# A gated linear-attention kernel: most of the first x rows transposed by the DMA engines instead of TensorE

## Chip, cores and metric

The kernel runs on one core of a Trainium2 chip. The metric is the device time of one execution in microseconds (us). Three runs of the kernel before gave a median of 188.91 us (188.75 to 189.58).

## The reference

Two linear-attention blocks A and B read the same input x (2048 rows, 640 columns, bf16) with their own weights, and a gate computed from x mixes their outputs. Cut to what matters:

```python
def block(x, wqkv, wo):                       # 32 heads of 20
    q, k, v = heads(x @ wqkv)
    phi = lambda t: where(t > 0, t + 1, exp(t)) + 1e-6
    pq, pk = phi(q), phi(k)
    kv = einsum("bhsd,bhse->bhde", pk, v)
    z  = einsum("bhsd->bhd", pk)
    num = einsum("bhqd,bhde->bhqe", pq, kv)
    den = einsum("bhqd,bhd->bhq", pq, z) + 1e-6
    return merge(num / den) @ wo

g = sigmoid((A_x * gate_w).sum(-1))
out = g * block(A_x, A_wqkv, A_wo) + (1 - g) * block(A_x, B_wqkv, B_wo)
```

## The kernel before

The 2048 rows of x are held twice in SBUF. `xn` has them as 16 chunks of 128 rows, rows on partitions. `xT` is x transposed, five slices of 128 columns by 2048 rows, columns on partitions. Products that sum over the 640 columns (k and q) read `xT`; products that sum over the rows (x transposed by phi(k), called g in the tile names) read `xn`.

The order of the work, for block A first and then for B, is: k for every chunk (`kA`: ten matmuls, two halves of 320 columns by five slices), phi on ScalarE and VectorE, q by weight slices (`qA`), the g products with Strassen-like sums, the normaliser, and then small weight products. At the end, pairs of row chunks make the output. Most of it lies in blocks under `tc.manual_schedule()`, where each engine's instructions stand in the order in which they are written.

The front of the kernel is where the change lies.

- **Loads (lines 113 to 141).** The first 512 rows of x are loaded by `load_x` as four chunks, `xn[:, 0]` to `xn[:, 3]`, in turn on SP's and ScalarE's queue. Chunk q holds the rows 4p + q (the view `xb0`), so these four chunks are interleaved. The k weights of A (`wkA`, five slices) come by `load_wk`, three transfers on SP and one on ScalarE. The q weights (`wqA`, lines 134 to 136) come in two transfers on SP. Behind all of these, SP issues 15 transposing transfers (line 139): for each of the row groups 512 to 1023, 1024 to 1535 and 1536 to 2047, five slices of 512 rows by 128 columns go straight into `xT`.
- **Warm-up and the gate weights (lines 168 to 178).** Seven matmuls on constants come first on TensorE. Then the gate weight row, five rows of 128, is transposed (`gcol`, line 174), copied by VectorE (`gsb`, line 176), and put by GpSimd (POOL) as a column 640 into each slice of `wkA` (line 178). The second half of each k product of A is therefore 321 columns wide, and its last column is the gate logit.
- **First k chunks (`k_first`, line 252).** For chunks 0 to 3, `x_transpose` (line 213) makes five TensorE transposes into PSUM and two VectorE copies into `xT`. All 20 transposes stand ahead of the 40 matmuls (`k_mm`, line 234), which go slice by slice: slice 0 for the four chunks, slice 1 for the four, and then slices 2 to 4 chunk by chunk, each followed by `k_done` (phi and the logit).
- **What follows (line 729).** q of rows 0 to 511 (`q_block` twice, `q_single`), k of chunks 4 to 7, q of rows 512 to 1023, k of chunks 8 to 15, and the remaining q. Chunks 4 to 7 read the first five of the 15 transposes. After these, SP loads `xn` for the chunks 4 to 15 (line 737), then `wv`, `wo` and B's k weights.
- **PSUM.** `ps_raw` hands out four slots of two banks each. A tile that takes a slot over waits for the readers of the tile before it. Before the change, the warm-up and the gate column are in slot 3, the transposes in slots 0 and 1, and the k products of chunks 0 to 3 in slots 2, 3, 0 and 1.
- **Output rows.** `rows_of` (line 598) sends chunks 0 to 3 to the interleaved rows and the others to plain ones.

Of the kernel before, what the change touches and what calls it, by code (L numbers as in the profile page):

```python
# [8 lines left out]
P = 128  # L9
FP32 = mybir.dt.float32  # L10
BF16 = mybir.dt.bfloat16
# [3 lines left out]
S, D, H = 2048, 640, 32  # L15
Dh = D // H
DT = D // P
ST = S // P
NB = 4
CB = 4  # L20
HB = 512
# [12 lines left out]
def kernel(  # L34
# [11 lines left out]
    nc = tc.nc  # L46
    x2 = A_x.flatten_outer_dims()
    out2 = out.flatten_outer_dims()
# [3 lines left out]
    wpool = ctx.enter_context(tc.tile_pool(name="wpool", bufs=1))  # L52
    work = ctx.enter_context(tc.tile_pool(name="work", bufs=2))
# [6 lines left out]
    def ps_raw(name, slot=None):  # L60

        if slot is None:
            slot = turn[0]
            turn[0] = (slot + 1) % 4
        return psum.tile([P, 4 * HB], BF16, tag=f"ps{slot}", name=name)

    def ps(name, slot=None):

        return ps_raw(name, slot).bitcast(FP32).rearrange("p (b n) -> p b n", b=2)

    xT = persist.tile([P, DT, S], BF16, name="xT")
    xn = persist.tile([P, ST, D], BF16, name="xn")
# [6 lines left out]
    ident = persist.tile([P, P], BF16, name="ident")  # L79
# [26 lines left out]
    wq_dram = [A_wqkv.rearrange("(c p) f -> p c f", p=P), B_wqkv.rearrange("(c p) f -> p c f", p=P)]  # L106
# [3 lines left out]
    nc.vector.memset(ones[:], 1.0)  # L110
    nc.vector.memset(KVT[:], 0.0)
    nc.vector.memset(lift[:], 1.0 + EPS)
    xb0 = x2[0:CB * P, :].rearrange("(p q) d -> p q d", q=CB)
    wk = [None, None]
    wv = [None, None]
    wq = [None, None]
    wk[0] = wpool.tile([P, DT, D + 16], BF16, tag="wk", name="wkA")
    def load_x(eng, lo, hi):
        eng.dma_start(out=xn[:, lo:hi, :], in_=xb0[:, lo:hi, :])

    def load_wk(eng, lo, hi):
        eng.dma_start(out=wk[0][:, lo:hi, 0:D], in_=wq_dram[0][:, lo:hi, D:2 * D])

    grow, logitT = R[0:DT, 0, 2, 0:P], R[:, 0, 1, 0:P]
    nc.scalar.dma_start(out=grow, in_=gate_w.rearrange("(c p) -> c p", p=P))
    load_x(nc.sync, 0, 1)
    load_x(nc.scalar, 1, 2)
    load_x(nc.sync, 2, 3)
    load_x(nc.scalar, 3, 4)
    load_wk(nc.sync, 0, 1)  # L130
    load_wk(nc.scalar, 1, 2)
    load_wk(nc.sync, 2, 3)
    load_wk(nc.sync, 3, DT)
    wq[0] = wpool.tile([P, DT, D], BF16, tag="wq", name="wqA")
    for lo, hi in ((0, 2), (2, DT)):
        nc.sync.dma_start(out=wq[0][:, lo:hi, :], in_=wq_dram[0][:, lo:hi, 0:D])
    for n in range(1, NB):
        for c in range(DT):
            nc.sync.dma_start_transpose(
                out=xT[:, c, n * HB:(n + 1) * HB], in_=x2[n * HB:(n + 1) * HB, c * P:(c + 1) * P]  # L140
            )


    make_identity(nc, ident[:])
    for r in range(4):
        rows = slice(32 * r, 32 * r + 32)
        nc.gpsimd.tensor_copy(out=I4[rows], in_=ident[rows, rows])
    nc.gpsimd.tensor_copy(
        out=spread[:].rearrange("p (h t) -> p h t", t=TW), in_=I4[:, :, None].to_broadcast([P, H, TW])
    )  # L150
    nc.gpsimd.tensor_tensor(
        out=I16[0:2 * ST], in0=ident[0:2 * ST, 0:ST], in1=ident[0:2 * ST, ST:2 * ST], op=ALU.add
    )
    nc.gpsimd.memset(maskE[:], 1.0)
    for sign, base in ((1, 0), (-1, Dh - 1)):
        nc.gpsimd.affine_select(
            out=maskE[:], in_=maskE[:], pattern=[[-sign * Dh, WB[0] // Dh], [0, Dh]],
# [3 lines left out]
    for sign, base in ((1, 0), (-1, TW - 1)):  # L161
        nc.gpsimd.affine_select(
            out=headE[:], in_=headE[:], pattern=[[-sign * TW, H]],
# [1 line left out]
        )  # L165


    raw = ps_raw("warm", 3)
    warm = raw.bitcast(FP32).rearrange("p (b n) -> p b n", b=2)
    one_l, one_r = [nc.const_aps.tensor(1.0, [P, n], BF16) for n in (P, HB)]  # L170
    for k in range(7):
        nc.tensor.matmul(warm[:, 0, :], lhsT=one_l, rhs=one_r, start=True, stop=True)  # L172
    gcol = raw[:, 2 * HB:2 * HB + DT]
    nc.tensor.transpose(out=gcol, in_=grow, identity=ident[0:DT, 0:DT])
    gsb = work.tile([P, DT], BF16, tag="rT", name="gsb")
    nc.vector.tensor_copy(out=gsb[:], in_=gcol)
    for c in (0, 1, 2, 4, 3):
        nc.gpsimd.tensor_copy(out=wk[0][:, c, D:D + 1], in_=gsb[:, c:c + 1])

    def by_group(dst, lhsT, src, h):  # L180

        for c in range(DT):
            for j in range(4):
                r0 = h * 2 * HB + j * RB
                nc.tensor.matmul(
                    dst[32 * j:32 * j + 32, :], lhsT=lhsT[:, c, :], rhs=src[:, c, r0:r0 + RB],
                    start=(c == 0), stop=(c == DT - 1), tile_position=(0, 32 * j),
                )
# [20 lines left out]

    def gate_done(b):  # L210
        nc.vector.tensor_scalar(ge[b][:], ge[b][:], 1.0, 1e30, op0=ALU.add, op1=ALU.min)

    def x_transpose(i, pt, cuts=(0, DT)):
        for c in range(DT):
            nc.tensor.transpose(out=pt[:, c * P:(c + 1) * P], in_=xn[:, i, c * P:(c + 1) * P], identity=ident[:])  # L215
        src = pt[:, 0:D].rearrange("p (c n) -> p c n", c=DT)
        for lo, hi in zip(cuts, cuts[1:]):
            nc.vector.tensor_copy(out=xT[:, lo:hi, i * P:(i + 1) * P], in_=src[:, lo:hi])  # L218

    def phi(dst, src, n, lifted=False, side=None):  # L220

        e = work.tile([P, src.shape[1], n], BF16, tag="e", name="e", bufs=3)
        nc.scalar.activation(out=e[:], in_=src, func=ACT.Exp)  # L223
        if side is not None:
            side()
        if lifted:
            nc.scalar.activation(out=dst, in_=src, func=ACT.Identity, bias=lift[:])
        nc.vector.tensor_scalar(e[:], e[:], 1.0, EPS, op0=ALU.min, op1=ALU.add)  # L228
        if lifted:
            nc.vector.tensor_tensor(out=dst, in0=dst, in1=e[:], op=ALU.max)  # L230
            return
        nc.vector.scalar_tensor_tensor(out=dst, in0=src, scalar=1.0 + EPS, in1=e[:], op0=ALU.add, op1=ALU.max)  # L232

    def k_mm(b, i, c, pt, hf):
        w = HF + (hf if b == 0 else 0)
        nc.tensor.matmul(  # L236
            pt[:, hf, 0:w], lhsT=xT[:, c, i * P:(i + 1) * P], rhs=wk[b][:, c, hf * HF:hf * HF + w],
            start=(c == 0), stop=(c == DT - 1),
        )

    def k_done(b, i, pt):
        side = (lambda: nc.scalar.copy(out=logit[:, i:i + 1], in_=pt[:, 1, HF:HF + 1])) if b == 0 else None
        phi(pk[:, i, :].rearrange("p (b n) -> p b n", b=2), pt[:, :, 0:HF], HF, side=side)

    def k_chunk(b, i, slot=None):
        pt = ps(f"k{'AB'[b]}", slot)
        for hf in range(2):
            for c in range(DT):
                k_mm(b, i, c, pt, hf)
        k_done(b, i, pt)  # L250

    def k_first():

        pts = [ps("kA", 2 + i) for i in range(2)]
        raw = [ps_raw("xt", i) for i in range(2)]

        def part(i, cs):
            for c in cs:
                for hf in range(2):
                    k_mm(0, i, c, pts[i], hf)  # L260

        for i in range(4):
            x_transpose(i, raw[i % 2][:, i // 2 * 2 * HB:], (0, 2, DT))
        for i in range(2):
            part(i, (0,))
        pts += [ps("kA", i) for i in range(2)]
        for i in range(2, 4):
            part(i, (0,))
        for i in range(4):
            part(i, (1,))  # L270
        for i in range(4):
            part(i, (2, 3, 4))
            k_done(0, i, pts[i])

    def mixed(t, m):
# [320 lines left out]
        nc.vector.tensor_tensor(out=pqT[b][:, m, :], in0=pqT[b][:, m, :], in1=rec, op=ALU.mult)  # L596

    def rows_of(i):
        n, q = divmod(i, CB)
        rows = out2[n * HB:(n + 1) * HB, :]  # L600
        return rows.rearrange("(p q) d -> q p d", q=CB)[q] if n == 0 else rows[q * P:(q + 1) * P, :]

    def prod(dst, left, right, i, first):

# [12 lines left out]
    class Pair:  # L617
# [7 lines left out]
        def store(self, k, lo=0, hi=D):  # L625
            eng = nc.scalar if self.last and k else nc.sync
            eng.dma_start(out=rows_of(self.i + k * (ST // 2))[:, lo:hi], in_=self.osb[k][:, lo:hi])
# [89 lines left out]
    with tc.manual_schedule():  # L717
        k_first()
# [3 lines left out]
    for h in range(2):  # L722
        for q in range(2):
            i0 = h * hc + q
            nc.gpsimd.tensor_copy(
                out=chosen[0:2 * ST, 2 * h + q, :].rearrange("p (j n) -> p j n", j=4),
                in_=I16[0:2 * ST, i0:i0 + hc - 1:2][:, :, None].to_broadcast([2 * ST, 4, 32]),
# [6 lines left out]
        q_single(0, DT - 1, n)  # L734
    for i in range(hc, ST - 2):
        k_chunk(0, i)
    for n in range(1, NB):
        nc.sync.dma_start(
            out=xn[:, n * CB:(n + 1) * CB, :], in_=x2[n * HB:(n + 1) * HB, :].rearrange("(q p) d -> p q d", p=P)
        )  # L740
    wv[0] = load_w(0, "v", nc.sync)
    load_wo(0, nc.sync)
# [5 lines left out]
    def bank(pool, name, n=1):  # L748
        return pool.tile([P, HB] if n == 1 else [P, n, HB], FP32, tag=name, name=name)

    with tc.manual_schedule():
# [31 lines left out]
        part = [slice(n * RB, (n + 1) * RB) for n in range(4)]  # L783
# [17 lines left out]
        with late_pool("single") as single:  # L801
# [6 lines left out]
            pts = [bank(single, f"s4{hf}")[:, 0:HF] for hf in range(2)]  # L808
# [21 lines left out]
        for i in range(1, half):  # L830
            p, after = pairs[i], pairs[i + 1] if i + 1 < half else None
# [9 lines left out]
            q = after if i + 2 < half else p if after is None else None  # L841
# [43 lines left out]
```

## Time and profile before

| | |
|---|---|
| median of 3 runs | 188.91 us |
| profiled execution | 188.86 us |
| its span, first to last instruction | 187.2 us |
| TensorE matmuls | 183.1 us busy (98%), 1426 instructions |
| TensorE weight loads (beside the matmuls) | 123.7 us (66%) |
| VectorE | 150.3 us (80%) |
| ScalarE | 76.3 us (41%) |
| GpSimd | 6.0 us (3%) |
| granted TensorE clock | 0.999 |
| DMA | 15.64 MB, mean 84 GB/s |

The span is the time between the first and the last instruction on the chip; the execution's own time has 1.7 us more around it. Busy shares say which engine could be the bound, and the chain that ended last says which one is. That chain is followed back from the last instruction: at each step to whatever released it, or to the instruction ahead of it on its engine. In the names, `PEld` is TensorE's weight load, and `SPq` and `ACTq` are the issuing of DMAs by SP and by ScalarE. A label such as L236 is a line of the kernel, and `xt` is the PSUM tile into which TensorE transposes.

### The profile page before, as it was taken

To read this page: it belongs to the slowest core of one execution; us is meant where nothing else is said; L and a number is where in the kernel's file an instruction comes from. 1 tells how busy PE (TensorE), PEld (TensorE's weight loads), DVE (VectorE), ACT (ScalarE), POOL (GpSimd) and SP (SyncE) were. 2 spreads that over 40 slices of the span, in tenths; PEclk is the share of its full clock that TensorE was granted. 3 is DMA by queue.
4 is the path that set the end of the run, shared out by engine and by line. 5 is a ranking of instruction groups with operands and counts; after the bars stand their busy time and mean duration, and the time that the engine had idled before them with its cause. 6 is when DMAs were issued, how large, how long until landed. Compare 5 with 4: busy or idle time off the path is not lost.

```text
span 187.2 us, 3548 instructions
## 1 busy us (share of the span) xinstructions
PE 183.1 (98%) x1426; PEld 123.7 (66%) x1431; DVE 150.3 (80%) x247; ACT 76.3 (41%) x124; POOL 6.0 (3%) x30
## 2 busy tenths in 40 slices
PE   8999999999999999999999999999999999999993
PEld 3765757765577677877775555576777776777772
DVE  1468868889998998799889998739699989787554
ACT  2065545547962501367674577432401611111120
POOL 7400000010000000000000000000000000000000
PEclk9999999999999999999999999999999999999999
DMA  5993449972040000011115000000533002311132
GB/s 169 323 165 74 99 98 352 322 164 101 9 170 0 0 4 0 0 36 33 55 38 190 8 0 0 0 4 0 179 98 77 4 0 91 123 67 65 50 107 70
DMA packets 19173, 15.64 MB, mean 84 GB/s; under 512 B 8916, under 2 KB 19028, under 8 KB 19156
## 3 DMA queue, kind: packets, MB, share of 16 engines
q1 hardware_dynamic: 18426, 14.75, 28.0%
q10 hardware_dynamic: 730, 0.66, 1.1%
q8 instruction: 11, 0.18, 0.4%
q14 instruction: 6, 0.05, 0.1%
HBM read 10.00 MB, written 3.44 MB: 72 GB/s over the span
## 4 chain that ended last, share of the span: by engine, by line
PE 96%; DVE 2%; issue 0%; ACT 0%; DVEq 0%; ACTq 0%
PE gs L367 16%; PE kA L236 12%; PE kB L236 12%; PE qB L285 12%; PE ox L607 6%; PE qA L285 6%; PE oy L607 5%; PE oz L607 5%; PE qA L296 5%; PE ow L607 3%; PE gA L340 2%; PE gB L340 2%; PE warm L172 2%; PE qA L306 1%; DVE osb L612 1%; PE xt L215 1%
## 5 line engine op out<-in xcount | busy, mean ns | idle before, releaser
L236 PEld LDWEIGHTS <-xT 128*128 128x128 bf16 x320 | 31.1, 98 | 12.4 <-DVE xT L218 0.2
L228 DVE TENSOR_SCALAR e<-e 128x640 bf16<-128x640 bf16 (+2 forms) x53 | 18.9, 357 | 8.3 <-ACT e L223 7.6
L236 PE MATMUL kB<-wkB,xT 128*128 128x320 bf16 x160 | 23.0, 299 | 0.0
L236 PE MATMUL kA<-wkA,xT 128*128 128x320 bf16 (+1 forms) x160 | 22.4, 300 | 0.0
L285 PE MATMUL qB<-xT,wqB 128*128 128x512 bf16 x98 | 21.7, 379 | 0.1
L223 ACT ACTIVATE e<-kB 128x640 bf16<-128x640 f32 x16 | 11.3, 705 | 18.8 <-PE kB L236 17.5
L285 PEld LDWEIGHTS <-wqB 128*128 128x128 bf16 x100 | 11.7, 117 | 9.8 <-issue 0.2
L223 ACT ACTIVATE e<-kA 128x640 bf16<-128x640 f32 x16 | 11.3, 705 | 13.4 <-PE kA L236 13.3
L232 DVE SCALAR_TENSOR_TENSOR pk<-kA,e 128x640 bf16<-128x640 f32 x16 | 13.2, 824 | 2.1 <-DVE e L228 0.2
L232 DVE SCALAR_TENSOR_TENSOR pk<-kB,e 128x640 bf16<-128x640 f32 x16 | 13.2, 825 | 1.7
L223 ACT ACTIVATE e<-qB 128x1024 bf16<-128x1024 f32 x10 | 10.3, 1025 | 8.7 <-PE qB L285 8.3
L223 ACT ACTIVATE e<-qA 128x1024 bf16<-128x1024 f32 (+1 forms) x11 | 10.4, 948 | 8.1 <-PE qA L296 5.1
L651 ACT COPY u<-ox 128x320 f32<-128x320 f32 x8 | 3.4, 427 | 21.8 <-PE ox L607 21.8
L367 PEld LDWEIGHTS <-S 128*128 128x128 bf16 x96 | 9.4, 98 | 3.6
L367 PEld LDWEIGHTS <-xn 128*128 128x128 bf16 x96 | 9.1, 98 | 4.0 <-issue 0.4
L285 PE MATMUL qA<-xT,wqA 128*128 128x512 bf16 x49 | 10.9, 379 | 0.1
L635 ACT COPY p1s<-ox 128x320 f32<-128x320 f32 x8 | 3.4, 427 | 16.5 <-PE ox L607 16.5
L607 PEld LDWEIGHTS <-xT 128*128 128x128 bf16 x85 | 8.0, 98 | 3.1 <-DVE xT L546 0.2
L607 PEld LDWEIGHTS <-pqTA 128*128 128x128 bf16 x85 | 7.9, 98 | 2.9 <-issue 0.2
L607 PEld LDWEIGHTS <-pqTB 128*128 128x128 bf16 x80 | 7.8, 98 | 3.0
L367 PE MATMUL gs<-pk,xn 128*128 128x320 bf16 x64 | 9.4, 300 | 0.0
L612 DVE TENSOR_TENSOR osb<-oz,u 128x320 bf16<-128x320 f32 (+1 forms) x18 | 8.0, 452 | 1.5 <-PE oz L607 0.8
(138 smaller groups left out, 293.6 us busy)
## 6 DMA issues: line engine op xcount, KB each, us to landing
out_dram<-osb SPq DMA_DIRECT2D x14, 160.0 KB, 1.8
xn<-in_A_x_dram SPq DMA_DIRECT2D x3, 640.0 KB, 6.6
wvA<-in_A_wqkv_dram SPq DMA_DIRECT2D x1, 800.0 KB, 10.6
wkB<-in_B_wqkv_dram SPq DMA_DIRECT2D x1, 800.0 KB, 4.5
wqB<-in_B_wqkv_dram SPq DMA_DIRECT2D x1, 800.0 KB, 4.6
MA<-ma_dram SPq DMA_DIRECT2D x1, 800.0 KB, 5.0
wvB<-in_B_wqkv_dram SPq DMA_DIRECT2D x1, 800.0 KB, 4.6
woB<-in_B_wo_dram SPq DMA_DIRECT2D x1, 800.0 KB, 5.7
```

Source lines behind the costliest of these rows:

```text
L172: nc.tensor.matmul(warm[:, 0, :], lhsT=one_l, rhs=one_r, start=True, stop=True)
L223: nc.scalar.activation(out=e[:], in_=src, func=ACT.Exp)
L228: nc.vector.tensor_scalar(e[:], e[:], 1.0, EPS, op0=ALU.min, op1=ALU.add)
L232: nc.vector.scalar_tensor_tensor(out=dst, in0=src, scalar=1.0 + EPS, in1=e[:], op0=ALU.add, op1=ALU.max)
L236: nc.tensor.matmul(pt[:, hf, 0:w], lhsT=xT[:, c, i * P:(i + 1) * P], rhs=wk[b][:, c, hf * HF:hf * HF + w], start=(c == 0), stop=(c == DT - 1),
L285: nc.tensor.matmul(pt[:, u, :], lhsT=mixed(wq[b][:, c, :], m), rhs=xT[:, c, n * HB:(n + 1) * HB], start=(c == 0), stop=(c == DT - 1),)
L296: nc.tensor.matmul(pt[:, u, :], lhsT=mixed(wq[b][:, c, :], m + u), rhs=xT[:, c, n * HB:(n + 1) * HB], start=(c == 0), stop=(c == DT - 1),)
L340: nc.tensor.matmul(pt[:, hf, 0:HF], lhsT=xn[:, i, c * P:(c + 1) * P], rhs=pk[:, i, hf * HF:(hf + 1) * HF], start=(i == 0), stop=(i == ST - 1),
L367: nc.tensor.matmul(pt[:, n, 0:HF], lhsT=left[:, i, n * P:(n + 1) * P], rhs=right[:, i, :], start=(first and i == 0), stop=(i == hc - 1), s ...
L607: nc.tensor.matmul(dst, lhsT=left[:, c, r0:r0 + P], rhs=right[:, c, :], start=(first and c == 0), stop=(c == DT - 1), skip_group_check=not ...
L612: nc.vector.tensor_tensor(out=dst, in0=acc, in1=sb, op=ALU.add)
L635: nc.scalar.copy(out=self.p1s[:], in_=self.at("x"))
```

## The change

Only chunk 0 of x is loaded at the start, on ScalarE's queue, and transposed on TensorE. Rows 128 to 511 come into `xT` by five transposing transfers, one for each slice of columns, 384 rows by 128 columns each, and these are the first five things that SP issues. `wkA` (in three transfers) and `wqA` (in two) go out on ScalarE's queue. The 15 transposes of the later rows stay on SP, behind the first five. `xn` of chunks 1 to 3 is loaded later by SP, with the other chunks. All chunks now hold plain rows, so the interleaved view and its store are gone.

In `k_first`, the five transposes of chunk 0 stand ahead of the gate weights' transpose. VectorE copies slices 0 and 1, then the gate column, then slices 2 to 4. The k matmuls begin with slice 0, first halves of chunks 1, 2, 3 and 0, then the second halves; then slice 1 for the four chunks; then chunk 0 to its end; then slices 2, 3 and 4 for chunks 1 to 3. The warm-up and the gate column take slot 1, the transposes slot 2; the k products keep their slots.

```diff
-    xb0 = x2[0:CB * P, :].rearrange("(p q) d -> p q d", q=CB)
-    def load_x(eng, lo, hi):
-        eng.dma_start(out=xn[:, lo:hi, :], in_=xb0[:, lo:hi, :])
+    def x_turned(c, lo, hi):
+        nc.sync.dma_start_transpose(out=xT[:, c, lo:hi], in_=x2[lo:hi, c * P:(c + 1) * P])
...
+    wq[0] = wpool.tile([P, DT, D], BF16, tag="wq", name="wqA")
+    nc.scalar.dma_start(out=xn[:, 0, :], in_=x2[0:P, :])
+    x_turned(0, P, HB)
     nc.scalar.dma_start(out=grow, in_=gate_w.rearrange("(c p) -> c p", p=P))
-    load_x(nc.sync, 0, 1)
-    load_x(nc.scalar, 1, 2)
-    load_x(nc.sync, 2, 3)
-    load_x(nc.scalar, 3, 4)
-    load_wk(nc.sync, 0, 1)
-    load_wk(nc.scalar, 1, 2)
-    load_wk(nc.sync, 2, 3)
-    load_wk(nc.sync, 3, DT)
-    wq[0] = wpool.tile([P, DT, D], BF16, tag="wq", name="wqA")
+    load_wk(nc.scalar, 0, 1)
+    x_turned(1, P, HB)
+    load_wk(nc.scalar, 1, 3)
+    x_turned(2, P, HB)
+    load_wk(nc.scalar, 3, DT)
+    x_turned(3, P, HB)
     for lo, hi in ((0, 2), (2, DT)):
-        nc.sync.dma_start(out=wq[0][:, lo:hi, :], in_=wq_dram[0][:, lo:hi, 0:D])
+        nc.scalar.dma_start(out=wq[0][:, lo:hi, :], in_=wq_dram[0][:, lo:hi, 0:D])
+    x_turned(4, P, HB)
     for n in range(1, NB):
         for c in range(DT):
-            nc.sync.dma_start_transpose(
-                out=xT[:, c, n * HB:(n + 1) * HB], in_=x2[n * HB:(n + 1) * HB, c * P:(c + 1) * P]
-            )
+            x_turned(c, n * HB, (n + 1) * HB)
...
-    raw = ps_raw("warm", 3)
+    raw = ps_raw("warm", 1)
...
-    nc.tensor.transpose(out=gcol, in_=grow, identity=ident[0:DT, 0:DT])
-    gsb = work.tile([P, DT], BF16, tag="rT", name="gsb")
-    nc.vector.tensor_copy(out=gsb[:], in_=gcol)
-    for c in (0, 1, 2, 4, 3):
-        nc.gpsimd.tensor_copy(out=wk[0][:, c, D:D + 1], in_=gsb[:, c:c + 1])
...
     def k_first():
 
-        pts = [ps("kA", 2 + i) for i in range(2)]
-        raw = [ps_raw("xt", i) for i in range(2)]
+        xt = ps_raw("xt", 2)
+        for c in range(DT):
+            nc.tensor.transpose(out=xt[:, c * P:(c + 1) * P], in_=xn[:, 0, c * P:(c + 1) * P], identity=ident[:])
+        nc.tensor.transpose(out=gcol, in_=grow, identity=ident[0:DT, 0:DT])
+        gsb = work.tile([P, DT], BF16, tag="rT", name="gsb")
+        src = xt[:, 0:D].rearrange("p (c n) -> p c n", c=DT)
+        nc.vector.tensor_copy(out=xT[:, 0:2, 0:P], in_=src[:, 0:2])
+        nc.vector.tensor_copy(out=gsb[:], in_=gcol)
+        nc.vector.tensor_copy(out=xT[:, 2:DT, 0:P], in_=src[:, 2:DT])
+        for c in range(DT):
+            nc.gpsimd.tensor_copy(out=wk[0][:, c, D:D + 1], in_=gsb[:, c:c + 1])
+        pts = {i: ps("kA", (2 + i) % 4) for i in (1, 2, 3, 0)}
+        for hf in range(2):
+            for i in (1, 2, 3, 0):
+                k_mm(0, i, 0, pts[i], hf)
...
-        for i in range(4):
-            x_transpose(i, raw[i % 2][:, i // 2 * 2 * HB:], (0, 2, DT))
-        for i in range(2):
-            part(i, (0,))
-        pts += [ps("kA", i) for i in range(2)]
-        for i in range(2, 4):
-            part(i, (0,))
-        for i in range(4):
+        for i in range(CB):
             part(i, (1,))
-        for i in range(4):
-            part(i, (2, 3, 4))
+        part(0, (2, 3, 4))
+        k_done(0, 0, pts[0])
+        for i in range(1, CB):
+            part(i, (2,))
+        for i in range(1, CB):
+            part(i, (3,))
+        for i in range(1, CB):
+            part(i, (4,))
             k_done(0, i, pts[i])
...
-    for n in range(1, NB):
+    for n in range(NB):
+        lo, hi = max(n * CB, 1), (n + 1) * CB
         nc.sync.dma_start(
-            out=xn[:, n * CB:(n + 1) * CB, :], in_=x2[n * HB:(n + 1) * HB, :].rearrange("(q p) d -> p q d", p=P)
+            out=xn[:, lo:hi, :], in_=x2[lo * P:hi * P, :].rearrange("(q p) d -> p q d", p=P)
         )
```

More of the change, by code (lines that the diff above doesn't have):

```diff
@@ L211, in gate_done @@
         nc.vector.tensor_scalar(ge[b][:], ge[b][:], 1.0, 1e30, op0=ALU.add, op1=ALU.min)
[L213 to L218, printed above, removed]
     def phi(dst, src, n, lifted=False, side=None):
@@ L598, in rows_of @@
     def rows_of(i):
-        n, q = divmod(i, CB)
-        rows = out2[n * HB:(n + 1) * HB, :]
-        return rows.rearrange("(p q) d -> q p d", q=CB)[q] if n == 0 else rows[q * P:(q + 1) * P, :]
+        return out2[i * P:(i + 1) * P, :]
     def prod(dst, left, right, i, first):
```

## The prediction

> **What bounds the kernel now.** I read the page first: share of busy time, then the chain that ended last.
>
> ```profile
> span 187.2 us, 3548 instructions
> ...
> PE 96%; DVE 2%; issue 0%; ACT 0%; DVEq 0%; ACTq 0%
> ```
>
> TensorE carries 96% of the chain, and its row of tenths is 8 or 9 in all slices but the last. So whatever TensorE does or waits for at the front moves the end one for one, as long as nothing behind it becomes late. The chain in order of time gives the front (start, length, what):
>
> ```profile
> 0.84 3.15 PE warm L172 x7
> 3.99 0.12 PE warm L174
> 4.11 0.65 PE xt L215 x5
> 4.75 0.04 issue
> 4.79 0.73 PE xt L215 x5
> 5.52 0.02 issue
> 5.54 0.57 DVE xT L218 x2
> 6.11 0.04 issue
> 6.15 0.44 PE xt L215 x5
> 6.59 5.54 PE kA L236 x40
> 12.14 0.22 PE qA L296
> ```
>
> The reader is to see that the 20 transposes through TensorE and the copies behind them fill the time from 4.11 to 6.59, and that the 40 matmuls of the first four k chunks then run without a gap into the q matmuls at 12.14. Next, the queue of SP in the timeline (start, time in issue):
>
> ```profile
> 3.14 1.98 SPq L136 DMA_DIRECT2D wqA<-in_A_wqkv_dram  x2
> 5.17 20.80 SPq L139 DMA_TRANSPOSE xT<-in_A_x_dram  x15
> ```
>
> Fifteen transposes of 512 rows: 1.26 us of issue each in the median, starting 1.30 to 1.31 apart (10.68, 11.99, 13.29). One is held for 2.25. An undisturbed one lands 2.8 after its issue begins; those at 10.68 and 13.29 took 3.2 and 3.3. Last, the windows table, whose last two columns are the DMA share (above 1 where packets overlap) and GB/s:
>
> ```profile
> 8.00:9.00 1.00, 1.00 (x10) 0.71 (x8) 0.00 (x0) 0.00 (x0) 0.00 (x0) 1.00 1.06 383
> 9.00:10.00 1.00, 1.00 (x10) 0.73 (x8) 0.00 (x0) 0.28 (x1) 0.00 (x0) 1.00 2.19 209
> 10.00:11.00 1.00, 1.00 (x9) 0.71 (x8) 0.39 (x2) 0.94 (x3) 0.00 (x0) 1.00 0.80 159
> 11.00:12.00 1.00, 1.00 (x10) 0.73 (x8) 0.99 (x2) 0.94 (x4) 0.00 (x0) 1.00 1.28 260
> ```
>
> At 8 to 9 nearly only plain loads move (383 GB/s), at 11 to 12 only transposes (260). From 9 to 11, where the tail of wqA meets the first transposes, both fall to 209 and 159. That fall is my main doubt.
>
> **TensorE's own work.** Removed are 15 transposes with their copies: 0.04 + 0.73 + 0.02 + 0.57 + 0.04 + 0.44 = 1.84 of the chain. The gate transpose (0.12) stays, now behind the five of chunk 0. The warm matmuls are unchanged, so: transposes 3.99 to 4.64, gate to 4.76, and kA can begin at 4.76 and not at 6.59, **1.83 sooner**.
>
> Added are waits. Before, the first copy began at 4.79, 0.04 after the fifth transpose's end. After, VectorE copies xT[0:2] at 4.68 (0.29), gsb (0.16) to 5.13, xT[2:5] (0.35) to 5.48. kA for rows 128 to 383 (slots 3 and 0) runs from 4.76 to 5.03. Rows 384 to 511 take slot 1, where the gate column lies, and wait for gsb: 0.14. Chunk 0 takes slot 2, that of the transposes, and waits for the last copy: 5.31 to 5.52, 0.21. Behind these two waits stands all of TensorE. The second halves, which need the gate column copied by POOL (five copies in 0.67, starting 0.07 after gsb in the trace), are hidden: column 0 is there at 5.4, wanted at 5.66. So **0.35 lost**, between 0 (copies may start before the fifth transpose) and 0.5 (each handover of 0.04 to 0.07 doubled). I take 0.35, which comes from the rows themselves. The 40 matmuls stay at 5.54, 0.14 each, so kA ends at 4.76 + 0.35 + 5.54 = 10.65 and not 12.14. Sum: **1.48 saved** by TensorE's order alone.
>
> **Transposes at the head of SP's queue.** The trace has no transpose of 384 rows. Bounds: three quarters of 1.31 (0.98), and 1.52 (the row at 7.86, 1.48 in issue with loads in flight, plus the gap of 0.04). I take 1.31, the nearest row unscaled. Issues begin at 0.81, 2.12, 3.43, 4.74 and 6.05; with 2.8 to 3.6 (the latter the one issued at 9.38) they land by 4.4, 5.7, 7.0, 8.3 and 9.65. By counting matmuls they are wanted at 4.76, 6.5, 8.16, 8.99 and 9.82. No wait, but only 0.2 to 0.4 of cover at the first and the last; at 0.98 the last lands 1.3 earlier, at 1.52 it lands at 10.5 and costs 0.7.
>
> The fifteen transposes of rows 512 to 2047 now begin at 7.36 (5.17 before). The fifth of them is issued at 12.6 and lands by 15.9; kA of chunk 4 wants it at 16.9 (10.95 + 5.39 of q matmuls + four kA). One more hold of 0.99, as the one at 13.29, is just covered. The tenth lands near 22 (wanted 27.2), the last near 28.5 (wanted 32.6). The four xn loads behind them carry 480 KB more (some 1.3 us at 370 GB/s), begin about 2 later, and the g matmuls read them at 49.9; xn's last part was in by 35.1 (issued at 27.2, 7.9 to land), so by some 39 now: cost nothing.
>
> **Loads on ScalarE's queue.** Seven issues at 0.37 to 0.56 each, back to back from 0.80: x chunk 0, the gate row, wkA in three, wqA in two, the last by about 4.9 (wqA's second issue sat 1.1 for an earlier transfer in the trace; one such wait is in). The activation table (1.28) then ends at 6.2, and the first Exp is wanted at 8.2: hidden, and worth up to 0.5 on the epilogue if it weren't. Chunk 0 lands 2.2 after its issue, at 3.0, wanted at 3.99; wkA's first slice goes out at 1.85, lands at 4.1 to 4.6, wanted 4.76.
>
> Whether bytes arrive in time: chunk 0, wkA and wqA are 1.80 MB, the five transposes 0.49 MB. At the pure rows, 1.80/383 + 0.49/260 = 6.6 us from the first bytes at 2.1, ending at 8.7. At 301 GB/s for loads (the mean of 3 to 7 in the windows view, with both queues at work), 6.0 + 1.9 = 7.9, ending at 10.0; the first 512-row transpose (131 KB, 0.5 us at 260) falls into that, so 10.5, and 0.6 to be seen: 11.1, up to 11.4 with gaps in issue. The q matmuls want wqA's second part at 11.08. At 160 GB/s throughout it would be 14.0. I take **0.3 lost** (bounds 0 and 2.9), by the row of 3 to 7, which alone shows two queues sharing.
>
> [...]
>
> **The sum.** The profiled execution took 188.86 with a span of 187.2. 188.86 − 1.83 + 0.35 + 0.3 = **187.7**. The median of the runs shown is 188.91, 0.05 above the profiled one, so the same sum holds for it.
>
> **Rivals.**
>
> 1. *No wait for loads, and early copies* (187.0 to 187.4): the pure rates hold. For it: 383 GB/s at 8 to 9. Against: it held there with one queue only.
>
> [...]
>
> 3. *The transposes themselves come late* (188.3): issue of 384 rows costs 1.52 or more, as at 7.86, 0.7 lost, or a hold falls among the first ten. At 2.25 each (the row at 13.29) the last would be 3.5 late.
>
> 4. *Slower: transposes hold up the loads beside them* (190.3). Place: 2 to 13 us, ScalarE's loads of wkA and wqA. For it: 209 and 159 GB/s at 9 to 11, share 2.19, so packets wait in the engines. Against: there both stood in one queue, the transposes behind loads that some engines had finished and others not. Price: at 160 GB/s wqA is in at 14.0 and not 11.1, 2.9 lost against 1.48 saved. It decides the sign when the loads average under 1.80 / (12.56 − 0.6 − 2.1) = 183 GB/s.
>
> That the change doesn't do what it says is unlikely: line 139 already issues such transposes and they run as DMA_TRANSPOSE.
>
> **Chances.** Forecast 0.44, rival 1 0.12, rival 2 0.14, rival 3 0.10, rival 4 0.20. Half a per cent, about what a measurement of this kernel can tell from no change, is 0.94 us, so the border is at 187.9. Faster: 0.38 of the forecast, all of 1, 0.02 of 2 = 0.52. Same: 0.06 + 0.12 + 0.06 of rival 3 + 0.02 of 4 = 0.26. Slower: 0.04 + 0.18 = 0.22. The range runs from 187.0 (rival 1) to 190.0, which leaves out the worse half of rival 4 and little else. The forecast's own range is 187.4 to 188.0.
>
> **What would show it.** In the chain after: transposes to 4.64, kA's start near 4.76, its 40 matmuls ending at 10.6 to 11, q without a wait of more than half a microsecond. In SP's queue: five transposes about 1.3 apart from 0.81. In the windows: if GB/s between 3 and 9 stays near 300 the loads are as priced; if it is under 200, rival 4. [...] The prediction is wrong if kA's first matmul waits past 5.2, or if any kA after chunk 3 waits for its transpose.

## The result and the profile after

The change makes the kernel slower: 197.97 us (median of 6 runs, 197.61 to 199.39) against 189.26 (6 runs), a ratio of 1.0458 with a 95% interval of 1.0408 to 1.0508. The forecast was 187.7 us, in a range of 187.0 to 190.0. The profiled execution took 198.0, its span 196.3, so 9.1 us more than before.

The page of the changed kernel, its span, TensorE's row and the chain by engine:

```profile
span 196.3 us, 3513 instructions
...
PE 185.4 (94%) x1411; PEld 123.2 (63%) x1416; DVE 148.9 (76%) x241; ACT 76.0 (39%) x124; POOL 6.0 (3%) x30
...
PE 88%; DMA 4%; SPq 4%; DVE 2%; issue 0%; ACT 0%; DVEq 0%; ACTq 0%
```

TensorE has 15 matmuls fewer and is busy for 2.3 us more, and the chain is no longer its own: a tenth of it is SP's issuing, DMA and VectorE. The chain in order of time shows where (start, length, what):

```profile
7.23 1.26 SPq L118
8.53 2.81 DMA xT<-in_A_x_dram
11.36 5.67 DMA wqA<-in_A_wqkv_dram
17.08 7.00 PE qA L293 x18
25.15 5.45 PE kA L221 x40
```

The second part of wqA was issued at 11.36, right behind the landing (8.53 + 2.81 = 11.34) of a transpose of rows 512 to 1023 that it has no use for. It took 5.67 to land, and 18 q matmuls behind it took 7.00 instead of 4.05. The timeline of ScalarE and TensorE from 1.9 on, with the idle time before each and what ended it:

```profile
1.90 2.20 ACTq L121 DMA_DIRECT2D wkA<-in_A_wqkv_dram  x3
9.64 2.10 ACTq L135 DMA_DIRECT2D wqA<-in_A_wqkv_dram  x2
11.78 1.28 ACT L208 ACT_TABLE_LOAD   x1 [11.78 <-DMA xT<-in_A_x_dram]
...
4.62 1.90 PE L221 MATMUL kA<-wkA,xT 128*128 128x320 bf16 x8
6.97 4.57 PE L221 MATMUL kA<-wkA,xT 128*128 128x320 bf16 x32 [0.45 <-DMA wkA<-in_A_wqkv_dram]
15.16 0.38 PE L293 MATMUL qA<-xT,wqA 128*128 128x512 bf16 x1 [3.62 <-DVE pk L217]
17.08 7.00 PE L293 MATMUL qA<-xT,wqA 128*128 128x512 bf16 x18 [1.54 <-DMA wqA<-in_A_wqkv_dram]
```

ScalarE's queue stood at wqA's two issues from 4.1 on, so its table load came at 11.78 and the first Exp at 13.07 (9.72 before). Hence the first q matmul waited for a PSUM slot until 15.16, and the next ones for wqA until 17.08, so the late Exp itself cost the chain nothing more. In the windows view the last three columns are granted clock, DMA share and GB/s:

```profile
13.00:15.00 2.00, 0.00 (x0) 0.00 (x0) 1.04 (x2) 1.99 (x7) 0.00 (x0) 1.00 1.10 134
15.00:17.00 2.00, 0.38 (x1) 0.12 (x1) 1.73 (x5) 0.90 (x4) 0.00 (x0) 0.80 1.03 256
17.00:20.00 3.00, 2.92 (x7) 1.04 (x8) 1.55 (x3) 0.00 (x0) 0.00 (x0) 0.50 0.74 156
20.00:24.00 4.00, 4.00 (x13) 1.59 (x12) 1.65 (x2) 1.02 (x1) 0.00 (x0) 0.62 0.44 98
```

TensorE had no matmul from 11.54 to 15.16 and next to none until 17.08. The granted clock fell to 0.50 at 16.2 and came back at 23.0, after 6.0 us of q matmuls (the trace's clock record; the windows show it as means). Before the fall, TensorE had been idle for 3.62 us, busy for 0.38 with one matmul, and idle for 0.7.

**The account.** kA's last matmul ended at 11.54 (12.14 before): 0.60 saved. From there to the k matmuls of chunk 4 it took 13.45, not 5.23: 2.95 of it slow clock, 5.27 waiting. Together 7.62 (24.99 against 17.37). 1.1 more is lost at 149, and 0.4 behind the last VectorE addition (cause open). The one at 149 is in the chain:

```profile
149.25 0.02 issue
149.27 0.90 DVE GT L419 x2
150.17 0.04 issue
150.21 0.92 PE mid L458 x20
```

Before, the `mid` matmuls followed the g products at 141.61 without a wait.

**What held wqA.** A completion counter is here a semaphore that a transfer raises when it has landed. In the program as built, SP's and ScalarE's transfers have eight of them in turn (numbers 100 and 103 to 109 in the traces before and after), in the order in which the scheduler placed them. In the front, a transfer that reuses a counter waits, on its issuing queue, until the counter's last transfer has landed. The kernel before has the same: there wqA's parts are tenth and eleventh, and wait for the counters of two x chunks (numbers 103 and 104). After the change SP issues transposes one after another from the start, and wqA's parts are 16th and 19th. The first waits for the fifth 384-row transpose (landed 9.63, wqA issued 9.64), the second for the second 512-row one (11.34, issued 11.36). The trace shows it directly, as it keeps the semaphore that each transfer raises and the one that its issue waits for: the fifth 384-row transpose and wqA's first part have number 109, the second 512-row one and wqA's second part 104. In the same way wkA's second part left at 3.10 and not at 2.25, when its queue was free: it waited for x chunk 0 (landed 3.09).

### The profile page after: what moved, and what is told of

Its sections match the earlier page's. It is cut to its first block, busy times and chain, and to the rows that moved or that the text cites. A ratio compares the mean times of both kernels' runs of the same rounds, so it can differ in the third digit from the quotient of the medians.

```text
span 196.3 us, 3513 instructions
## 1 busy us (share of the span) xinstructions
PE 185.4 (94%) x1411; PEld 123.2 (63%) x1416; DVE 148.9 (76%) x241; ACT 76.0 (39%) x124; POOL 6.0 (3%) x30
## 4 chain that ended last, share of the span: by engine, by line
PE 88%; DMA 4%; SPq 4%; DVE 2%; issue 0%; ACT 0%; DVEq 0%; ACTq 0%
PE gs L364 16%; PE kB L221 11%; PE qB L282 11%; PE kA L221 8%; PE qA L293 6%; PE ox L602 6%; PE qA L282 5%; PE oy L602 5%; PE oz L602 5%; SPq L118 4%; DMA wqA<-in_A_wqkv_dram 3%; PE ow L602 2%; PE gA L337 2%; PE gB L337 2%; DMA xT<-in_A_x_dram 1%; PE qA L303 1%
## 5 line engine op out<-in xcount | busy, mean ns | idle before, releaser
L221 PE MATMUL kA<-wkA,xT 128*128 128x320 bf16 (+1 forms) x160 | 23.2, 305 | 0.4 <-DMA wkA<-in_A_wqkv_dram 0.4
L282 PEld LDWEIGHTS <-wqB 128*128 128x128 bf16 x100 | 11.8, 118 | 9.8 <-issue 0.2
L293 PE MATMUL qA<-xT,wqA 128*128 128x512 bf16 x38 | 11.8, 471 | 5.2 <-DVE pk L217 3.6
L208 ACT ACTIVATE e<-qB 128x1024 bf16<-128x1024 f32 x10 | 10.2, 1023 | 8.7 <-PE qB L282 8.4
L293 PEld LDWEIGHTS <-wqA 128*128 128x128 bf16 x40 | 5.0, 128 | 11.6 <-issue 6.1
L282 PE MATMUL qA<-xT,wqA 128*128 128x512 bf16 x49 | 10.9, 379 | 0.1
```

What stands on the lines that cost most here:

```text
L221: nc.tensor.matmul(pt[:, hf, 0:w], lhsT=xT[:, c, i * P:(i + 1) * P], rhs=wk[b][:, c, hf * HF:hf * HF + w], start=(c == 0), stop=(c == DT - 1),
L282: nc.tensor.matmul(pt[:, u, :], lhsT=mixed(wq[b][:, c, :], m), rhs=xT[:, c, n * HB:(n + 1) * HB], start=(c == 0), stop=(c == DT - 1),)
L293: nc.tensor.matmul(pt[:, u, :], lhsT=mixed(wq[b][:, c, :], m + u), rhs=xT[:, c, n * HB:(n + 1) * HB], start=(c == 0), stop=(c == DT - 1),)
```

## Experiments

Two theories. **Counters:** wqA is late since its issue waits for other transfers' counters. **Transfers** (rival 4 of the prediction): loads and transposes slow each other on the DMA engines whenever they meet, so wqA would be late however early it is issued. A third question is the 1.1 us at 149.

**1 and 2: where the PSUM slots lie.** `ps_raw` places a slot when it is first touched, 3, 2, 0, 1 before and 1, 2, 3, 0 after. The late tiles near the end lie over them in that order, so after the change the second `mid` tile covers slot 0, which VectorE reads last. One edit, made in both kernels:

```diff
+    for k in (3, 2, 0, 1):      # in the kernel before: (1, 2, 3, 0)
+        ps_raw("first", k)
     raw = ps_raw("warm", 1)     # in the kernel before: 3
```

> The changed kernel with nothing altered but where the four PSUM slots lie: they are touched in the order 3, 2, 0, 1 at the start, as the kernel before does. Bank theory: the 1.1 us that the tail loses (B's small products wait for VectorE's last two G additions) goes, since the second of the late tiles no longer lies over slot 0; 196.9 us against 198.0. Rival, that VectorE is late there as a result of the late front: no change, 198.0.

> The kernel before with its PSUM slots touched in the order 1, 2, 3, 0, as the changed kernel does. Bank theory: it gains the same wait on VectorE near the end, 1.1 us, 190.1 against 189.0. Rival (late front): no change.

The changed kernel with the old places: 197.05 us, ratio 1.0445 (1.0425 to 1.0466). The total alone doesn't tell it from 1.0458, as wqA's second part left 1.5 later here (12.90); but its chain has no DVE between the g products and `mid`. The kernel before with the new places: 189.94, ratio 1.0090 (1.0023 to 1.0157) to the kernel before at 188.66 (a wide interval, as two of its five executions took 192.2 and 192.3), and in its waits of TensorE (us in total, times, longest) one that it never had:

```profile
PE mid L463 <- DVE GT L424: 1.0, 1, 1.0
```

So the wait of 1.0 to 1.1 us belongs to the slots' new order, not to the transposes: the waits in the two traces show it, the totals alone would not.

**3: one transfer out of the counters.**

```diff
-    nc.scalar.dma_start(out=grow, ...)
+    nc.gpsimd.dma_start(out=grow, ...)
```

> The changed kernel with the 1.2 KB gate row loaded on GpSimd's queue, which takes one transfer out of the row of eight completion counters that SP's and ScalarE's transfers share in turn. Counter theory: wqA's two issues now share counters with the third transpose (landed at 8.6) and with the first 512-row one (10.1), not with the fifth and seventh, so they leave at about 8.7 and 10.2 instead of 9.64 and 11.36, and the time falls by 1 to 2 us. Transfer theory (loads are slow beside transposes whenever they are issued): wqA lands at about 17 as before and the time stays.

196.04 us, ratio 1.0412 (1.0349 to 1.0475), about 1.9 less than the change, with intervals that overlap. wqA's first part left at 6.58 and not at 8.7: its counter was that of the third transpose, which had landed sooner. The second left at 11.97 and not at 10.2: its counter was that of the transpose issued at 7.25, which now met wqA's first part and landed 4.70 later, at 11.95. Both issues sit where the new counters put them; the landings that they wait for had moved. So the counters hold for the issues. They don't explain the time: wqA's second part landed at 16.67 against 17.03, only 0.4 earlier, as the transfers' theory had it, and the 18 q matmuls took 4.96 and not 7.00, since the slow clock lasted 3.4 us here (0.66 in the mean of 15 to 20, 1.00 in the windows beside it) and not 6.8. Some 2.0 of the fall come from the clock.

**4: wqA issued early.** The gate row as in 3, and

```diff
-    load_wk(nc.scalar, 1, 3)
+    load_wk(nc.scalar, 1, DT)
...
-    load_wk(nc.scalar, 3, DT)
...
-    for lo, hi in ((0, 2), (2, DT)):
-        nc.scalar.dma_start(out=wq[0][:, lo:hi, :], ...)
+    nc.scalar.dma_start(out=wq[0][:], in_=wq_dram[0][:, :, 0:D])
```

> As the run with the gate row on GpSimd, and wkA in two transfers, wqA in one, so that wqA's counter is that of wkA's first slice, landed at 4.6. Counter theory: wqA leaves at about 4.7, is in by 11.5, the q matmuls follow kA within 1 us at full clock, the first Exp is no longer held; 198.0 less 7 to 8, so 190 to 191 with the bank wait of 1.1 still in. Transfer theory: 1.62 MB of weights beside the transposes at about 160 GB/s or less are not in before 14 to 15, and the time stays above 193.

192.33 us (190.64 to 193.09), ratio 1.0178 (1.0122 to 1.0233): 5.6 less than the change. In the profiled execution (190.64) wqA left at 4.31 and q started behind kA without a gap, at 12.15 and at full clock. This is the fastest of the four executions; two of the others had a lower granted clock (0.987 and 0.991). What waited now was kA, for a transpose (timeline of TensorE):

```profile
10.50 1.81 PE L219 MATMUL kA<-wkA,xT 128*128 128x320 bf16 x12 [0.85 <-DMA xT<-in_A_x_dram]
12.15 4.48 PE L291 MATMUL qA<-xT,wqA 128*128 128x512 bf16 x19
```

The fourth transpose, issued at 4.64, landed at 10.46, 5.82 later. Most of the loss was wqA's held issue, with the waiting and the slow clock behind it; the rest moved from the loads to the transposes.

**5: the clock.** In the changed kernel, ahead of the last `k_done` of `k_first`:

```diff
+            if i == 3:
+                for k in range(96):
+                    nc.tensor.matmul(pts[3][:, 0, 384:HB], lhsT=one_l, rhs=one_r[:, 0:P], start=True, stop=True)
```

> The changed kernel with 96 matmuls of 128 columns on constants, into unused PSUM columns, between the k and the q matmuls (about 5 us at full clock, where TensorE idles until wqA is there). Clock theory: the granted clock, 0.62 at 15 to 20 and 0.70 at 20 to 25 in the changed kernel, stays at 1.0, the first 18 q matmuls take 4.05 and not 7.0, and 2.5 to 3 us come back: 195.2. Rival, that these matmuls are slow because their weights or rows still arrive: no gain, 198.0.

The clock held (windows; 0.62 and 0.70 in the changed kernel), and the 18 q matmuls took 4.08:

```profile
15.00:20.00 5.00, 3.95 (x58) 3.38 (x56) 3.85 (x8) 2.69 (x8) 0.00 (x0) 1.00 1.35 199
20.00:25.00 5.00, 5.00 (x26) 2.74 (x25) 2.31 (x4) 2.21 (x3) 0.00 (x0) 1.00 0.51 107
```

But the whole took 197.13 (195.98 to 198.09), ratio 1.0438 (1.0381 to 1.0496), not told apart from the change's 1.0458. In the profiled execution wqA landed 2.6 later than in the changed kernel (19.60 against 17.03), which ate the 2.9. That the slow clock came from the waiting and cost the q matmuls 2.9 is shown; that the whole would gain as much isn't, as the best of the four executions gained 2.0.

**6: the 512-row transposes held back.** As 4, with the old slot order, and SP waiting for wqA ahead of the fifteen (the loads behind them are moved along):

```diff
+    held = scratch.tile([P, 16], BF16, name="held")
+    nc.sync.dma_start(out=held[:], in_=wq[0][:, DT - 1, D - 16:D])
     for n in range(1, NB):
```

> As the run with wqA issued early, with the four PSUM slots in the order of the kernel before, and with the 15 transposes of rows 512 to 2047 (and the loads behind them) held back on SP until wqA is in. The first five transposes and the weights are alone on the DMA engines. If the 512-row transposes are what delays the front's transfers: the fourth and fifth 384-row transposes land by 8 and wqA by 9.5. If it is the weights themselves beside the first five: the fourth still lands after 9.5 (10.46 in the run with wqA issued early). In either case chunk 4's k waits for its own transposes until about 19 to 20, and the whole takes 191 to 193.

One execution, 191.96. wqA left at 3.30 here and landed at 12.1. The five transposes landed 3.9, 6.6, 9.1, 7.9 and 6.6 after their issues. So the five and the weights alone are enough: the third, issued at 3.35, landed at 12.49 and set kA. The granted clock fell here too, from 8.4 to 11.8 if it fell to 0.50 as in the change (means of 0.84 at 5 to 10 and 0.82 at 10 to 15), though the longest idle time ahead of it was 1.8 us; kA waited for the third transpose all the same.

**7: both repairs together** (4 with the old slot order).

> wqA issued early and the PSUM slots in the order of the kernel before: the two repairs together. Counter and bank theories: 1.0 to 1.1 us under the run with wqA issued early (190.6 to 193.1 in four executions), so 189.5 to 192, with no wait of TensorE on VectorE near the end. Not under the kernel before (188.7) by more than 0.3, as kA's end at 12.3 is then set by the fourth transpose's landing.

191.99 (191.74 to 192.64), ratio 1.0180 (1.0150 to 1.0210). The wait near the end is gone, but kA waited for the fourth transpose until 12.68, so the total tells nothing new of the 1.0. The sum is inconclusive, and this is not a better kernel. Its front issues the same transfers as run 4, and the fourth transpose landed 8.05 after its issue instead of 5.82: so much do executions differ.

**8: the loads moved alone**, in the kernel before: `load_wk` and the wqA loads on `nc.scalar`, nothing else.

> The kernel before, with wkA and wqA issued on ScalarE's queue and nothing else altered; x is still loaded in four chunks and transposed on TensorE. Counter theory: SP's 15 transposes now start at 1.7 and share the counters in turn with ScalarE's loads, wqA's second part waits for a transpose (the one fourth in SP's row) and leaves no earlier than 8 to 10, q waits and the clock falls: 4 us or more over the kernel before, 193 to 198. If the loss needs the 384-row transposes, this one stays within 1 us of 188.7.

One execution, 192.07, 3.4 over the kernel before (188.72). Chain:

```profile
4.29 4.24 DMA xT<-in_A_x_dram
8.53 0.02 issue
8.55 0.38 ACTq L136
8.93 0.04 issue
8.97 6.55 DMA wqA<-in_A_wqkv_dram
```

It was wqA's first part that waited, not the second as expected, and 3.4 us is under the 4 expected; the clock held (1.00 in all windows to 30). But no 384-row transpose is needed for the loss: loads on one queue and a run of transposes on the other are enough.

**9 and 10: wqA at two better places**, both with the old slot order. In 9 SP issues wqA behind the five transposes; in 10 the gate row is on GpSimd, wkA in its three parts, and wqA is one transfer on ScalarE.

```diff
-    for lo, hi in ((0, 2), (2, DT)):
-        nc.scalar.dma_start(out=wq[0][:, lo:hi, :], ...)
     x_turned(4, P, HB)
+    for lo, hi in ((0, 2), (2, DT)):
+        nc.sync.dma_start(out=wq[0][:, lo:hi, :], ...)
```

> The changed kernel with wqA issued by SP, behind the five 384-row transposes and ahead of the fifteen, and with the PSUM slots in the order of the kernel before. No load of ScalarE waits for a transpose's counter, only wkA moves beside the first five, and wqA has its queue's place ahead of the 512-row transposes. Counter theory and transfer theory agree that wqA leaves at 7.3; with transfers as in the changed kernel (five transposes in by 9.6, 800 KB at 300 to 380 GB/s after 8.7) wqA is in at 11.5 to 12.5, kA ends at 11.5 to 12, and the time is 188.5 to 190. If it is over 191, mixing costs more than I think.

> The changed kernel with the gate row on GpSimd's queue, wqA in one transfer on ScalarE's queue, wkA in its three, PSUM slots as in the kernel before. wqA's counter is that of the third transpose (landed at 8.65 in the changed kernel), so it leaves at 6.6 to 8.7. Counter theory: one wait less than the run with the gate row on GpSimd (196.0), the clock holds, 190 to 192. Transfer theory: wqA beside the 512-row transposes takes 6 to 8 us to land (5.7 for 480 KB in the changed kernel), so 192 to 194.

9 took 190.78 (190.46 to 191.16), ratio 1.0101 (1.0059 to 1.0142); 10 took 191.28, ratio 1.0113 (1.0071 to 1.0154). Both are the best of the transposed versions, and both are about 1% slower than the kernel before. In 9, kA waited for wkA's last part until 9.79: against what was expected, its issue waited for a transpose (what released ScalarE is a transfer of xT), was over at 5.32 and not at 4.10 as in the change, and kA could go on 4.5 later. And q waited for wqA until 13.92, 6.0 after the issue of its second part:

```profile
9.79 3.16 PE L223 MATMUL kA<-wkA,xT 128*128 128x320 bf16 x22 [1.54 <-DMA wkA<-in_A_wqkv_dram]
13.92 4.08 PE L295 MATMUL qA<-xT,wqA 128*128 128x512 bf16 x18 [0.54 <-DMA wqA<-in_A_wqkv_dram]
```

**11: transposes and weights kept apart.** A measurement on the kernel of 6: ScalarE waits for the fifth transpose ahead of wkA.

```diff
+    first = scratch.tile([P, 16], BF16, name="first")
+    nc.scalar.dma_start(out=first[:], in_=xT[:, DT - 1, HB - 16:HB])
     load_wk(nc.scalar, 0, 1)
```

> A measurement, not a candidate: the weights wait until the five 384-row transposes have landed, and the other transposes until wqA is in, so that transposes and loads hardly meet. If meeting is what makes both slow: each of the five lands 2.8 to 3.0 after its issue (the last near 9), and wkA and wqA, 1.64 MB, move at 350 GB/s or more, in some 4.7 us. If the transposes are slow by themselves, the third to fifth take 4 us or more even here; if the loads are slow on ScalarE's queue, they stay under 300 GB/s. The whole is 8 us or more slower than the kernel before, as nothing overlaps.

The five landed 3.5, 2.8, 3.1, 2.5 and 2.5 after their issues, the last at 8.48. The weights, issued from 8.86, were in by 16.35 and moved at 374 GB/s from 12 to 14 (windows: of this run, then, of run 9, a stretch in which both kinds meet):

```profile
12.00:14.00 2.00, 1.49 (x6) 0.70 (x5) 0.00 (x0) 0.00 (x0) 0.00 (x0) 0.50 1.03 374
```

```profile
12.00:14.00 2.00, 1.46 (x10) 0.78 (x9) 1.26 (x3) 1.55 (x5) 0.00 (x0) 1.00 1.64 119
```

Neither is slow by itself here, and neither queue is: it is the meeting. Apart, the two take until 16, and 197.05 in all. Why they slow each other so is open: the share of 1.64 at 119 GB/s, against 1.03 at 374, says that packets are under way for longer, not what they wait for. The trace's packets say the same of the loads: in the stretch of run 11 a packet took 55 ns in the mean (601 packets at that share), and in the changed kernel from 13 to 15, where both kinds move at 134 GB/s, one of 1280 bytes took 146 in the mean, though 55 in the median.

## Why the prediction was wrong

- **Right:** the place of TensorE's start and of SP's issues. Transposes began at 3.78 and kA at 4.62 (4.76 forecast). SP's first five issues stood 1.26 to 1.29 apart (1.31). 384 rows are as dear in issue as 512 (1.24 against 1.26). The rows behind them came in time.
- **Wrong in TensorE's own part:** kA ended at 11.54 and not at 10.65, so 0.60 was saved and not 1.48. The two PSUM waits (0.35) didn't show. But "the 40 matmuls stay at 5.54, 0.14 each" failed: until 5.9 they started 0.27 apart, then 0.14, which cost 0.65. TensorE runs at half speed at first, in the kernel before too (warm-up matmuls 0.43 apart there); kA, starting earlier, fell into it. The prediction's own rows had the sign (7 warm-up matmuls in 3.15, 0.45 each, against 0.225 for q matmuls of the same 512 columns). The clock column reads 1.00 there because the trace's clock record only begins at 5.97 (5.98 after the change). The ninth matmul then waited 0.6 for wkA's second part, which its counter had held.
- **The step that failed** is "Loads on ScalarE's queue": seven issues back to back, the last by about 4.9, with "one such wait" in it. The fourth already stood until 3.10. The trace of before had the sign, wqA's second issue standing 1.1 us for an x chunk, and I carried its length over and not its rule. I didn't ask which transfer would be in that place after the change. wqA's issues left at 9.64 and 11.36 and not by 4.9, and with the slow clock behind them the k matmuls of chunk 4 began 7.6 late (24.99 against 17.37). The semaphores in the trace and the issue times of runs 3, 4 and 8 show that the counters did it; issuing wqA at 4.31 (4) gave back 5.6.
- **Undersized: meeting transfers.** I took 0.3, by the row at 301 GB/s with two queues of loads, and put the fall to 209 and 159 down to a single queue's order. With wqA issued at 4.31 and 4.07, q began at 12.3 and 14.5 (chains of runs 4 and 7) and not at 10.95, so the meeting cost 1.4 to 3.6 more, kA's own small waits included. The best versions (9, 10) still lose 1.9 and 2.4 against the kernel before, 3 or more against the forecast; part of this is wqA's later issue. Runs 6 and 11 show that the meeting is what slows both. Rival 4 had the place and the sign and was given 0.20. In the changed kernel itself most of the loss was not its mechanism, since wqA was late in leaving. It named only the loads, and the transposes suffer as much (9.1 instead of 3.1 us in runs 6 and 11). Rival 2, given 0.14, supposed a way of sharing the engines that no run shows; what the runs show is when transposes land beside loads (3.9 to 9.1 after their issues in run 6).
- **Hidden work exposed.** I called the table load hidden until 8.2. It stands behind the issues on ScalarE's queue and came at 11.78, so the epilogue and PSUM were late as well; wqA, later still, hid the cost.
- **Not thought of:** the clock (2.95 us) and the slot order (1.1 us, runs 1 and 2). The diff renames the slots in plain sight; I checked who waits for a slot in the front, and not what lies over it later.
- **The signs.** That q would wait no more than half a microsecond was the one that spoke. The 212 GB/s from 3 to 9 lie between the two values named. The two that were to call the prediction wrong stayed quiet: kA's first matmul didn't wait past 5.2, and no kA after chunk 3 waited for its transpose. No kA waited for the third transpose either, by luck: it landed at 8.68 and not by 7.0, but kA was late itself.

## What to carry to other kernels

Before moving a transfer to another queue, list the completion counters that it shares, in the order of the built program, and ask which landing its issue will wait for; what stands behind it on that queue waits too (here the table load, until 11.78). Price transposes beside loads by a stretch in which the two meet (119 GB/s in run 9), not by the sum of their rates alone (260 and 383 in the kernel before). Look at the spacing of TensorE's first matmuls before pricing what moves to the front (here 0.27 until 5.9, then 0.14). If TensorE will idle for some microseconds, allow for a slow clock behind it (here 3.62 idle, then 0.50 for 6.83); and if PSUM tiles are named anew, look at what is laid over them at the end.

## What was new of the hardware

- Transposes of 384 rows: 2.5 to 3.5 us to land with no weights beside them (run 11), 3.9 to 9.1 beside 1.64 MB of weights (run 6). Loads alone moved 374 GB/s (run 11, 12 to 14); loads and transposes together 107 to 238 in the stretches 6 to 8, 8 to 10 and 12 to 14 of runs 9 and 10, but 332 and 333 from 10 to 12.
- The issue of a transpose hardly depends on its rows: 1.24 us for 384, 1.26 for 512 (the change).
- TensorE's first matmuls run at half speed (512 columns 0.43 us apart against 0.22 later). The speed changes where the trace's clock record begins: at 5.97 in the kernel before (TensorE's transposes 0.11 apart until 5.8, 0.06 from 6.15), at 5.98 after the change (k matmuls 0.27 apart, then 0.14). Full speed can come earlier: TensorE's five transposes at 3.8 took 0.45 in run 11 and 0.74 in the change.
- The granted clock stood at 0.50 for 6.83 us in the change, for about 3.4 in runs 3 and 6 (worked out from their windows' means, for a fall to 0.50), and in run 11 from 8 to 16 at least. The length of one idle time doesn't settle it: 1.8 us among short bursts came before the fall in run 6, and 2.5 us in run 10 brought none (1.00 from 2 to 16).
